# A two-layer block (linear attention and gated MLP, twice) on one core: the hand-written order, engine choices and buffer slots replaced by another set

## Chip, core and metric

The kernel runs on one core of one Trainium2 chip. The core has five engines that run side by side: TensorE (PE, matmuls, with its weight loads PEld), VectorE (DVE), ScalarE (ACT), GpSimd (POOL) and SyncE (SP, which issues DMAs). The metric is the device time of one execution in microseconds (us). Every time below is from the profiler's trace of one execution, or from the timed runs where that is said.

## What is computed

A sequence of 2048 tokens with 512 features goes through attention, MLP, attention, MLP, with the same weights in both layers, everything in bfloat16:

```
x = A_x                                   # (2048, 512)
for layer in (0, 1):
    n = layernorm(x);  q, k, v = split(n @ wqkv)          # 32 heads of 16
    pq, pk = q @ w_phi, k @ w_phi                         # by head, 16 x 16
    phi_q = concat(softmax(pq), softmax(-pq))             # 32 features a head
    phi_k = concat(softmax(pk), softmax(-pk))
    kv = sum over tokens of phi_k x v;  z = sum of phi_k
    x = x + ((phi_q @ kv) / (phi_q @ z + 1e-6)) @ wo
    n = layernorm(x)
    x = x + (relu(n @ W_gate) * (n @ W_up)) @ W_down      # 1376 wide
```

The attention is linear: kv and z need all 16 tiles of keys, and no query can be finished before that. This is the one place in each layer where everything waits for everything.

## The kernel before

**Tiles.** The tokens are 16 tiles of 128 (T). x stays in SBUF in four tensors X0 to X3 for the whole run. The weights are loaded once; w_phi is folded into the key and query weights at the start ("turn", L440, transposes a block of Wk on PE, "wT" copies it, "fold", L448, multiplies it with a block-diagonal w_phi, "W2" copies the result; Wq is transposed by DMA, L435, instead). Both copies are L425 on ACT or L426 on DVE, as are most moves out of PSUM.

**Operations of the first layer, by name and line.** For each tile:

- stats and aggr (L477, L478, DVE), ln and rstd (L485, L487, ACT), xnA (L495, DVE: the normalised tile), xnTA (its transpose: on PE, L466, for the first four tiles, with a copy on ACT; by DMA, L461, for the others).
- K (L535, PE, four matmuls of 128x512): exponentials of plus and minus the result into a buffer ek (L538, ACT, two), sums by head (sk, L546, DVE), one over the sum by lnk and rk (L555, L558, ACT), scaling in two halves, "phi" (L509, on POOL or DVE).
- V (L541, PE, four matmuls) and its copy vext (L425 on ACT or L426 on DVE).
- kvz (L570, PE, eight small matmuls) adds the tile to kv and z in one PSUM buffer q.
- Q (L597, PE, four matmuls), then as for keys: Eq (L600, ACT, two), sq (L603, DVE), lnq and rq (L606, L608, ACT), two halves "phq" (L509, POOL or DVE), and a DMA transpose fq (L611, SP).

When all 16 kvz are done, R and Rz (L582, L587, DVE) build the matrix for the queries. Then, for each tile: erq (L622, PE, eight small matmuls into the same buffer q, which must be free again), lnd and rden (L629 and L633 on ACT, or one reciprocal L631 on DVE), o (L636, DVE), oT (transposed by PE or DMA), proj (L645, PE), resS (L649, DVE: x plus the result), xc (L665, DVE: centred) and xnTB (transposed), ssq (the square's sum, L671 on ACT or L673 on DVE).

The MLP follows in blocks of 1, 1, 2, 4, 4, 2, 2 tiles (1, 1, 2, 4, 4, 2, 1, 1 in the second layer): GU (L698, the last 96 columns), G and Up (L722, PE), rg (L726, ACT: relu), ru (L741 a copy on ACT and then L730 on DVE, or L739 on DVE alone) giving hT, down (L762, PE) and resB (L769, DVE). Tiles of the second layer start their keys while the MLP of the first is still running.

**What sets the order.** Nothing is scheduled at run time. The function builds a list of 1880 operations, ops. ORDER is a list of their numbers: the operations are issued in this order, and each engine takes its own in the order in which they stand there, one after the other. PLACE holds one character for each operation that has a choice of engine, and a "1" swaps it to the other one. SLOTS gives the buffer that each operation takes from its pool: 6 PSUM banks b, one PSUM buffer q, 21 buffers ek, 7 fq, 3 xn and so on. IDLE gives, for the first PE operations, how many idle matmuls of zeros by zeros (L419) stand before each; eight more of them, "warm", begin the program.

```
    order = arrange(ops)
    with tc.manual_schedule():
        fill = iter(IDLE)
        for o in order:
            if o.eng == "PE":
                idle(next(fill, 0))
            o.emit()
```

A wait thus comes from a dependency on another engine, from a buffer that is still in use, or from an instruction ahead on the same engine. DMAs are issued by SP (two at the start by ACT) in order as well; each waits for the landing of the one eight before it.

A number behind a name below counts the operations of that name as they are built (K0 to K15 are the keys of the first layer, K16 to K31 of the second; xnTA has two numbers where PE transposes, one for the matmuls and one for the copy; fold0 to fold3 belong to Wk, fold4 to fold7 to Wq; phi0 and phi1 are the halves of tile 0).

Of the kernel before, what the change touches and what calls it, by code (L numbers as in the profile page):

```python
# [142 lines left out]
class K:  # L143
# [9 lines left out]
    "0101110100000000001100000100110001000011010001111000000011001101010101001001001000101001111111011010"  # L153
    "1011110000000100000001001101000000000111011001011111010111000101001100000101111101001100001101010100"
    "1111111110101010010001000011000100000000101100101010100001001100011100010000110011001101000110111001"
    "010110010110111001110100110100000"
)
SLOTS = (
    "0001425210034050000151131234202310332121143404550125d3104c02302b3020a12113g533004002394131703202e141"
    "5i022124504f013k03583226105214413624335a011h100b033c05053623122j214910170400020501131002000245011020"  # L160
    "2500001142021002010100203200101143020002012105002004314023104g13300215112012320410311e34110200400450"
    "10205113120513d5100i42221240121321402422031200151030231042100142131004133610104f33242541002510104203"
    "51101520500512052130201550414201515300804024k2232c4020121152143124212004023502a533344112050010024104"
    "02024213011055002220j4203h05133317362b222f1506242i013a114023391638231c343e352k221d014g10011500020514"
    "0010124302000012011021450000121302100024010021050012201000011011521101530431102000005112025421011101"
    "0213125200125020013101050032154203115143114220221100253415210511200211401013403005210402213013222420"
    "500210300512431510432512113015114024105320310110512400202"
)
IDLE = (
    0, 0, 0, 0, 0, 0, 0, 0, 0, 0, 2, 0, 4, 0, 0, 0, 0, 0, 0, 0, 0,  # L170
# [708 lines left out]
```

## Time and profile before

| | |
|---|---|
| median of 3 runs | 377.31 us (377.04 to 377.71) |
| span of the profiled execution, first to last instruction | 375.3 us |
| instructions | 7459 |
| PE busy | 364.6 us (97%), 2793 matmul records |
| PEld, DVE, ACT, POOL busy | 216.6 (58%), 285.1 (76%), 209.7 (56%), 93.5 us (25%) |
| granted TensorE clock | 1.000 |
| bytes read from HBM, written | 7.91 MB, 2.10 MB |

The time of the profiled execution is its span and what lies around it; only the span is recorded for it. The median of the timed runs is 2.0 us above this span.

Busy is the union of an engine's instructions over the span. A matmul's record includes its drain, and matmuls overlap, so PE can be busy while it makes no headway; starts in the timeline show that better. Some 40 matmul records are missing (2793 of 2833).

The landings at the start, from the trace (issue, landing, us): X tile 0 0.74, 3.56; first half of Wk 0.74, 4.08; second half 1.19, 4.97; w_phi 1.25, 5.16; wv 1.75, 5.94 and 2.30, 6.74; X tiles 1, 2, 3 2.81 to 3.80, 7.15, 7.50, 7.87; then two tiles (256 KB) each about 0.75 after the last, to 12.36.

### The profile page before, as it was taken

The page shows a single profiled execution, that of the slowest core. Times are in us where ns is not written, and L with a number is a line of the kernel's source. Part 1 is how long each engine was busy: PE and PEld are TensorE (multiplying, and loading weights), DVE is VectorE, ACT ScalarE, POOL GpSimd, SP SyncE. Part 2 cuts the span into 40 slices and gives each one's busy share as a digit, 9 for nine tenths or more (in the row PEclk, how much of TensorE's full clock was granted, in tenths as well). Part 3 has the DMA queues.
Part 4 walks back from the last instruction along what each step waited for, and adds up shares of the span by engine and source line. Part 5 has one row for each costly group of instructions (what it writes and reads, how often), then busy time and mean ns, then how long its engine had stood idle before and what let it go on. Part 6 is the DMA issues. An engine that isn't in the chain of part 4 may idle for free.

```text
span 375.3 us, 7459 instructions
## 1 busy us (share of the span) xinstructions
PE 364.6 (97%) x2793; PEld 216.6 (58%) x2833; DVE 285.1 (76%) x596; ACT 209.7 (56%) x553; POOL 93.5 (25%) x91
## 2 busy tenths in 40 slices
PE   8989997999999999999999999999999999999996
PEld 4534454868554554466476555587745444558585
DVE  6999999999998673685767999999994755543322
ACT  6989999746464532265155499973425323414031
POOL 0377984341010102001004269774000000000000
PEclk9999999999999999999999999999999999999999
DMA  8858844769814221012020102968664120211110
GB/s 256 191 139 175 312 58 85 123 113 132 164 36 84 47 53 31 11 25 56 9 56 2 29 2 57 141 93 142 143 132 85 31 56 2 56 29 51 42 51 30
DMA packets 93444, 31.21 MB, mean 83 GB/s; under 512 B 85248, under 2 KB 92384, under 8 KB 93408
## 3 DMA queue, kind: packets, MB, share of 16 engines
q1 hardware_dynamic: 92992, 30.34, 39.5%
q8 instruction: 22, 0.36, 0.4%
q10 hardware_dynamic: 416, 0.39, 0.3%
q14 instruction: 14, 0.11, 0.1%
HBM read 7.91 MB, written 2.10 MB: 27 GB/s over the span
## 4 chain that ended last, share of the span: by engine, by line
PE 90%; ACT 6%; DVE 1%; POOL 1%; issue 1%; DVEq 0%; another core or an unknown queue 0%
PE b L722 37%; PE b L762 20%; PE b L645 7%; PE b L541 6%; PE b L535 6%; PE b L597 6%; PE b L698 3%; PE q L622 2%; PE q L570 2%; ACT ek L600 1%; POOL ek L509 1%; ACT ek L538 1%; PE q L419 1%; DVE sq L603 1%; ACT hT L425 1%
## 5 line engine op out<-in xcount | busy, mean ns | idle before, releaser
L722 PE MATMUL b<-xnTB,wgu 128*128 128x128 bf16 (+2 forms) x1200 | 149.6, 279 | 0.0
L722 PEld LDWEIGHTS <-wgu 128*128 128x128 bf16 x1200 | 97.1, 98 | 43.6
L509 POOL TENSOR_TENSOR ek<-ek,sk 128x512 bf16<-128x512 bf16 x47 | 51.0, 1109 | 135.5 <-ACT sk L558 108.2
L726 ACT ACTIVATE gu<-b 128x512 bf16<-128x512 f32 (+1 forms) x83 | 47.8, 580 | 64.9 <-PE b L722 64.6
L762 PE MATMUL b<-wd,hT 128*128 128x512 bf16 (+2 forms) x350 | 81.3, 372 | 0.7
L762 PEld LDWEIGHTS <-hT 128*128 128x128 bf16 (+1 forms) x363 | 34.6, 98 | 35.9 <-DVE hT L739 0.2
L509 POOL TENSOR_TENSOR ek<-ek,sq 128x512 bf16<-128x512 bf16 x38 | 42.0, 1127 | 32.6 <-ACT sq L608 18.0
L739 DVE TENSOR_TENSOR hT<-gu,b 128x512 bf16<-128x512 bf16 (+1 forms) x44 | 29.6, 676 | 18.5 <-PE b L722 16.9
L546 DVE TENSOR_REDUCE sk<-ek 128x64 f32<-128x1024 bf16 x32 | 38.7, 1210 | 5.3 <-ACT ek L538 5.2
L538 ACT ACTIVATE ek<-b 128x512 bf16<-128x512 f32 x64 | 35.9, 598 | 9.2 <-PE b L535 8.0
L603 DVE TENSOR_REDUCE sq<-ek 128x64 f32<-128x1024 bf16 x32 | 38.2, 1207 | 0.3 <-POOL ek L509 0.3
L600 ACT ACTIVATE ek<-b 128x512 bf16<-128x512 f32 x64 | 36.1, 623 | 0.6 <-PE b L597 0.5
L730 DVE TENSOR_TENSOR hT<-gu 128x512 bf16<-128x512 bf16 (+1 forms) x39 | 16.7, 429 | 22.5 <-ACT gu L741 22.3
L769 DVE SCALAR_TENSOR_TENSOR X<-b,rsB,X 128x512 bf16<-128x512 f32 (+1 forms) x33 | 23.2, 726 | 13.5 <-PE b L762 13.4
L645 PE MATMUL b<-wo,oT 128*128 128x512 bf16 x118 | 31.2, 379 | 1.2 <-ACT oT L425 0.7
L535 PE MATMUL b<-Wk,xnTA 128*128 128x512 bf16 x122 | 31.4, 379 | 0.3
L541 PE MATMUL b<-wv,xnTA 128*128 128x512 bf16 x124 | 31.0, 379 | 0.4 <-ACT xnTA L425 0.2
L597 PE MATMUL b<-Wq,xnTA 128*128 128x512 bf16 x121 | 30.5, 379 | 0.3
L741 ACT CAST gu<-b 128x512 bf16<-128x512 f32 (+1 forms) x39 | 21.7, 558 | 15.0 <-PE b L722 14.6
L649 DVE SCALAR_TENSOR_TENSOR X<-b,X 128x512 bf16<-128x512 f32 x32 | 21.8, 682 | 3.5 <-PE b L645 3.4
L636 DVE TENSOR_TENSOR o<-q,rd 128x512 bf16<-128x512 f32 x32 | 21.9, 685 | 0.8 <-ACT rd L633 0.6
L477 DVE BATCH_NORM_STATS2 bstA<-X 128x6 f32<-128x512 bf16 x32 | 21.0, 681 | 1.9 <-DMA X<-in_A_x_dram 1.8
(71 smaller groups left out, 349.1 us busy)
## 6 DMA issues: line engine op xcount, KB each, us to landing
out_dram<-X SPq DMA_DIRECT2D x15, 128.0 KB, 1.7
X<-in_A_x_dram SPq DMA_DIRECT2D x6, 256.0 KB, 4.8
wgu<-in_B_W_gate_dram SPq DMA_DIRECT2D x4, 344.0 KB, 4.0
wgu<-in_B_W_up_dram SPq DMA_DIRECT2D x4, 344.0 KB, 3.6
wd<-in_B_W_down_dram SPq DMA_DIRECT2D x5, 256.0 KB, 3.6
wv<-in_A_wqkv_dram SPq DMA_DIRECT2D x2, 256.0 KB, 4.3
wo<-in_A_wo_dram SPq DMA_DIRECT2D x4, 128.0 KB, 3.2
fq<-ek SPq DMA_TRANSPOSE x32, 3.3
```

Of the source, the lines that this page charges most:

```text
L509: e.tensor_tensor(out=out().rearrange("p g s (h f) -> p (g s h) f", f=DH)[:, lo:lo + n], in0=ek.t[:].rearrange("p g s (h f) -> p (g s h) f ...
L535: k = op("PE", mm(4, 512), due, lambda: [nc.tensor.matmul(kp.t[:], lhsT=xnTA[c][:, i, b, :], rhs=Wk2[:, b, :], start=(b == 0), stop=(b == ...
L538: e = [op("ACT", act(512), due, lambda s=s: nc.scalar.activation(out=ek.t[:, :, s, :], in_=kp.t[:].rearrange("p (g e) -> p g e", e=GQ), fu ...
L541: v = op("PE", mm(4, 512), due_v, lambda: [nc.tensor.matmul(vp.t[:], lhsT=xnTA[c][:, i, b, :], rhs=wv[:, b, :], start=(b == 0), stop=(b == ...
L546: a = op("DVE", SUM16, due, lambda: nc.vector.tensor_reduce(out=sk.t[:, row, :], in_=ek.t[:].rearrange("p g s (h f) -> p (g s h) f", f=DH) ...
L597: q = op("PE", mm(4, 512), due, lambda: [nc.tensor.matmul(qp.t[:], lhsT=xnTA[c][:, i, b, :], rhs=Wq2[:, b, :], start=(b == 0), stop=(b == ...
L600: e = [op("ACT", act(512), due, lambda s=s: nc.scalar.activation(out=ek.t[:, :, s, :], in_=qp.t[:].rearrange("p (g e) -> p g e", e=GQ), fu ...
L603: a = op("DVE", SUM16, due, lambda: nc.vector.tensor_reduce(out=sq.t[:], in_=ek.t[:].rearrange("p g s (h f) -> p (g s h) f", f=DH), axis=A ...
L645: a = op("PE", mm(4, 512), due + 3, lambda j=j, yp=yp: [nc.tensor.matmul(yp.t[:], lhsT=oT.t[:, j, b, :], rhs=wo[:, b, :], start=(b == 0), ...
L722: nc.tensor.matmul(ps.t[:, q * W:(q + 1) * W].rearrange("p (i t) -> p i t", t=P), lhsT=wgu[:, s, b, g * P:(g + 1) * P], rhs=xT.t[:, 0:n, b ...
L726: nc.scalar.activation(out=gu.t[:, 0, 0:cols], in_=gp.t[:, 0:cols], func=AF.Relu)
L762: nc.tensor.matmul(yp.t[:, 0:c1 - c0], lhsT=h.t[:m, f * W + i * P:f * W + (i + 1) * P], rhs=wd[:m, f, c0:c1], start=(f == 0), stop=(f == N ...
```

## The change

Only the four constants PLACE, SLOTS, IDLE and ORDER are replaced. The operations, their shapes, the pools and the function that builds them are the same. All of the strings differ; here is their beginning, and IDLE in full (in the changed file the lines below the constants have numbers 3 lower; this text keeps those of the kernel before, but lines quoted from a profile after the change have the new ones):

```diff
 PLACE = (
-    "0101110100000000001100000100110001000011010001111000000011001101010101001001001000101001111111011010"
+    "0101010100000100001100001000110000101110000110000000000110100111000100000000000010001000000001010011"
...
 SLOTS = (
-    "0001425210034050000151131234202310332121143404550125d3104c02302b3020a12113g533004002394131703202e141"
+    "0001245203033002000554133113211224414011381200321310i0311h22300d3403e3120214002k23221c4415a402212041"
...
 IDLE = (
-    0, 0, 0, 0, 0, 0, 0, 0, 0, 0, 2, 0, 4, 0, 0, 0, 0, 0, 0, 0, 0,
+    0, 3, 0, 3, 0,
 )
...
 ORDER = (
-    0, 24, 16, 3, 25, 17, 18, 20, 1, 4, 29, 22, 19, 21, 23, 26, 2, 5, 28, 6, 7, 46, 8, 9, 47, 48, 10, 49, 30, 50,
+    17, 29, 16, 18, 0, 26, 22, 46, 19, 47, 3, 8, 82, 30, 9, 1, 4, 32, 10, 2, 83, 48, 31, 100, 49, 50, 33, 84, 85, 34,
...
```

What the numbers say, worked out from the lists. PE's first groups:

```
before: warm turn0 turn1 turn3 xnTA0 turn2 fold0 fold3 fold1 fold2 (2 idle) V0 K0 (4 idle) xnTA6 xnTA4 xnTA2 V3 K1 K2
        V2 V1 K3 kvz0 fold4 fold6 fold5 fold7 K4 kvz1 V4 V5 K5 kvz3 kvz2 V13 K13 Q3 K12 Q2 V12 kvz5 ...
after:  warm (3 idle) turn0 turn1 (3 idle) turn2 xnTA0 turn3 fold0 fold2 xnTA4 fold1 fold3 xnTA6 V0 V2 V3 K0 xnTA2 fold6
        K3 fold4 K1 fold7 K2 V1 fold5 K5 K4 Q2 Q3 Q1 V4 V12 kvz0 K13 Q0 V13 K12 V5 kvz2 K8 ...
```

PE's groups from the last kvz of the first layer to its first gate group G0:

```
before: kvz11 Q7 Q15 Q10 erq0 Q14 Q9 oT0 proj0 erq1 xnTB0 erq2 oT2 G0
after:  kvz7 Q12 erq0 Q7 Q15 oT0 Q9 proj0 erq1 Q14 xnTB0 oT2 erq2 G0
```

The first DMAs of SP, after the first half of Wk: before w_phi, wv, wv, X tiles 1, 2, 3, then the other 12 tiles in pairs, then four transposes of Wq; after X tiles 2 and 3, w_phi, X tiles 4 and 5, wv, wv, X tile 1, X tiles 12 and 13, two transposes of Wq, four X tiles, two more transposes of Wq, a transpose of an xn, and the last four X tiles. On DVE the zero memset comes first instead of third, and the statistics of tiles 0, 2 and 3 all stand ahead of the first normalisation xnA0, where only tile 0's did.

Engines by PLACE, for the whole program:

| operation | before | after |
|---|---|---|
| vext on ACT / DVE | 19 / 13 | 25 / 7 |
| key halves phi on POOL / DVE | 47 / 17 | 46 / 18 |
| query halves phq on POOL / DVE | 38 / 26 | 51 / 13 |
| lnd and rden on ACT / rden on DVE | 15 / 17 | 19 / 13 |
| ssq on ACT / DVE | 21 / 11 | 17 / 15 |
| ru on ACT / DVE | 39 / 44 | 36 / 47 |
| copies oT, xnTB on ACT / DVE | 8 / 0 | 4 / 4 |
| copies W2 on ACT / DVE | 6 / 2 | 7 / 1 |

In the second layer the last erq of the queries stands after 331.8 us of PE work instead of after 292.9 (by matmul lengths); the last groups of PE (G81, Up81, down90 to down98) are nearly in the same order.

More of the change, by code (lines that the diff above doesn't have):

```diff
@@ L152 @@
 PLACE = (
-    "0101110100000000001100000100110001000011010001111000000011001101010101001001001000101001111111011010"
-    "1011110000000100000001001101000000000111011001011111010111000101001100000101111101001100001101010100"
-    "1111111110101010010001000011000100000000101100101010100001001100011100010000110011001101000110111001"
-    "010110010110111001110100110100000"
+    "0101010100000100001100001000110000101110000110000000000110100111000100000000000010001000000001010011"
+    "0101010111111000110001001100101011011011011010001101001110100001110001111001110110100101001101110111"
@@ L157 @@
+    "1110101111011010101001100000101100000000001000010010101010111101010111010010101000000010100010101000"
+    "101000011011110010110110001101101"
 )
 SLOTS = (
-    "0001425210034050000151131234202310332121143404550125d3104c02302b3020a12113g533004002394131703202e141"
-    "5i022124504f013k03583226105214413624335a011h100b033c05053623122j214910170400020501131002000245011020"
-    "2500001142021002010100203200101143020002012105002004314023104g13300215112012320410311e34110200400450"
-    "10205113120513d5100i42221240121321402422031200151030231042100142131004133610104f33242541002510104203"
@@ L163 @@
[L163 to L167, printed above, removed]
+    "0001245203033002000554133113211224414011381200321310i0311h22300d3403e3120214002k23221c4415a402212041"
@@ new lines @@
+    "0j10011222391007014522263313154g042f26243130103j224a0308351c245b064i215d1000000001121202000202011020"
+    "0400001103021002250100204300101124020000121001000005015313514k44202211112212004023204h51000400310132"
+    "13140053204120841341011112311105115224002023100305123024522315131005f3325451020552316000001210503004"
+    "025225514510201400312000014153021j4210a54215c3321d4200111122102131235124033100e5033i3311040022055001"
+    "0521502324222k2421012342292507144e02523323310g062b2005340702201526030c113g265f301h044922011223020414"
@@ L168 @@
+    "0010101402000203011021240000100202100235010021040010401020031111411500042312103001205510002511311221"
+    "3410422011305400022002101043150250114031034113012232040521110501113011113413403414520120201424302420"
+    "320200300021412520431543115110011220512200000520231542103"
 )
 IDLE = (
-    0, 0, 0, 0, 0, 0, 0, 0, 0, 0, 2, 0, 4, 0, 0, 0, 0, 0, 0, 0, 0,
+    0, 3, 0, 3, 0,
 )
```

181 rows, old and new, of the table ORDER are left out of this document.

## Prediction

> **What bounds the kernel now.** I read first the stages (busy time of each engine by stretch), because the shares of the whole span hide where time is lost. Columns: PE, PEld, DVE, ACT and POOL busy us with their instructions, granted clock, DMA share, GB/s.
>
> ```profile
> 0.00:10.00 10.00, 8.30 (x53) 4.22 (x55) 6.27 (x24) 6.42 (x13) 0.70 (x6) 1.00 0.83 263
> 10.00:20.00 10.00, 9.47 (x72) 4.89 (x71) 9.86 (x21) 9.97 (x31) 4.20 (x4) 1.00 0.87 205
> 20.00:30.00 10.00, 8.57 (x58) 4.11 (x59) 10.00 (x23) 8.77 (x29) 7.44 (x7) 1.00 0.56 135
> 30.00:60.00 30.00, 29.61 (x225) 15.17 (x228) 29.92 (x38) 29.41 (x84) 24.52 (x22) 1.00 0.68 162
> 60.00:65.00 5.00, 3.29 (x46) 2.22 (x45) 4.96 (x8) 4.91 (x18) 2.12 (x2) 1.00 0.54 103
> 65.00:372.00 307.00, 305.26 (x2352) 185.97 (x2382) 223.44 (x486) 150.21 (x384) 54.51 (x50) 1.00 0.34 64
> ```
>
> From 65 us to the last matmul at 372 PE alone is full and sets the time. What can be won lies ahead of 65, where ACT and DVE are as full as PE and PE has holes. Next PE's own waits (total, times, longest):
>
> ```profile
> PE q L570 <- POOL ek L509: 1.5, 3, 0.7
> PE q L419 <- DVE zero L396: 1.3, 1, 1.3
> PE b L466 <- DVE xn L665: 0.8, 1, 0.8
> PE b L645 <- ACT oT L425: 0.7, 1, 0.7
> PE q L622 <- DVE o L636: 0.2, 1, 0.2
> ```
>
> The waits name three places: kvz (L570) behind POOL, the start, and the step from attention to MLP. Busy PE includes the drain of a matmul, so I took the lost time from the starts in the timeline: a 512-column matmul follows the last after 0.216, a 128-column one after 0.056, a kvz or erq one after 0.032; what is longer is lost. That gives 1.34 before the first matmul, 1.7 in the eight warm-up matmuls (0.427 each instead of 0.216), 1.7 in small gaps up to 12.3, 2.3 in kvz between 19.3 and 25.0, and 2.7 between 59.3 and 63.8. After that, nothing over 0.1.
>
> The first gate group (L722, "G0") starts at 64.25. PE work ahead of it: 49 groups of 4x512 at 0.862 = 42.2, 19 of eight kvz/erq at 0.254 = 4.8, 19 of 4x128 at 0.223 = 4.2, 14 warm-up and idle ones at 0.216 = 3.0; sum 54.2. So **10.0 us are lost ahead of G0**, and this is the number that the change must alter.
>
> **Why they are lost.** For ACT, DVE and POOL I take as an instruction's engine time the stretch from the end of the one before it to its own end, averaged over the trace (the timeline shows four exponentials L538 in 2.04, four casts L425 in 2.05: 0.51 each). ACT work up to the cast that G0 reads, in the kernel's order: 32 exponentials of keys 16.4, 32 of queries 16.0, 16 pairs lnk/rk 6.1, 9 pairs lnq/rq 3.0, 11 vext casts 5.6, 6 casts of Wk/Wq 2.9, 10 other casts 5.1, 10 ln/rstd pairs 3.4, table and two DMA issues 2.2, two lnd/rden 0.7, one square 0.7: 62.1. ACT idle before that: 0.74, 1.58 (for the first statistics) and 0.2, so 2.5. Sum 64.6, against 64.25 seen. ACT sets G0; the kvz gaps and the long chain at 59 lie in its shadow in part.
>
> **The change, part by part.** It removes and adds no matmul: the same 2833, six of them idle, and the same 54.2 ahead of G0. Counts that do move: vext on ACT 19 to 25, rden/lnd on ACT 15 to 19, square on ACT 21 to 17, relu copies on ACT 39 to 36, query halves (phq) on POOL 38 to 51, key halves 47 to 46. By the engine times explained above, DVE's whole work falls from 285 to 277 and ACT's from 211 to 209; POOL's rises by 12.6.
>
> *Front.* Three idle matmuls now precede the first transpose and three the third. The zero memset is first on DVE (0.27 earlier), so: warm-up 1.15 to 4.54, three idle ones to 5.35, first transpose 5.35 instead of 4.72, its cast (L425) 5.74 instead of 5.22. Its weights landed at 4.1, so these idles cost ACT 0.9 of idle in place of 0.2. On DVE the statistics of two more tiles stand before the first normalisation (L495, at 5.09 before); their loads are moved to second and third on SP, where the trace's landings (256 KB each 0.75) put them near 4.9 and 5.3. So L495 comes at 6.5 and its transpose at 7.0, not 5.56; ACT meanwhile has casts to do and stays busy. ACT idle becomes 3.4. On SP the moved loads pull wv to about 7 and 7.7 (5.9, 6.7 before); V0 starts near 9.8 by ACT's casts, so that is hidden. Two later X loads stand behind Wq's transposes and an xnTA transpose; the queries of early tiles now fill PE there.
>
> *kvz.* kvz0 goes from PE's 22nd group to its 33rd, behind three queries. POOL's first half waits for rk0: ACT sum 11.9 + 2.5 = 14.4 before (seen: 14.5), now 18.5 + 3.4 = 21.9. Two halves end at 24.0, when PE has just reached kvz0. The 2.3 lost in kvz go, but the later POOL start is paid below.
>
> *ACT up to G0.* 24 exponentials of queries instead of 32 (-4.0), 6 lnq/rq pairs (-1.0), one lnd/rden (-0.4), no square (-0.7), 13 vext (+1.0), 7 W casts (+0.5): 57.5, with 3.4 idle 60.9, so 6.7 lost. The tightest place is two groups earlier: proj0 has 51.5 of PE work and 55.3 of ACT before it, 58.7, so **7.2 lost**. DVE up to the first centred tile falls from 59.6 to 53.8 and is no bound.
>
> *The step to MLP.* Before, proj0 follows its transpose at once, and xnTB0 follows proj0 after one erq (0.25), though L649 and L665 take 1.1; seen: 0.84, 1.0, and 0.36 and 0.34 beside. Now a query group (0.86) stands in each of these places; the same rows leave 0.2 at xnTB0 and 0.2 to 0.4 at oT1/erq2.
>
> *POOL.* Up to the second half that erq1's transpose needs, POOL now does 31 halves without a rest: 21.9 + 31 x 1.04 + 2.0 of waits for ACT's rk/rq (running sum) = 56.2, and 3.3 for the DMA transpose: 59.5. erq1 has 52.4 of PE work before it: 7.1 lost, the same as ACT. But POOL has no slack left for this:
>
> ```profile
> 20.86 4.10 POOL L509 TENSOR_TENSOR ek<-ek,sk 128x512 bf16<-128x512 bf16 x4 [1.02 <-ACT sk L558]
> ...
> 39.12 4.62 POOL L509 TENSOR_TENSOR ek<-ek,sk 128x512 bf16<-128x512 bf16 x4
> 41.12 0.68 DVE L509 TENSOR_TENSOR ek<-ek,sk 128x512 bf16<-128x512 bf16 x1
> ```
>
> Four halves take 4.10, and 4.62 where DVE starts the same operation just ahead of one of them; single POOL halves go from 1.057 to 1.36 to 1.57 there. Five DVE halves now stand among POOL's last ten before erq1. None hit: 0; all hit: 5 x 0.5 = 2.5; I take two, 1.0. [...]
>
> *Later stages.* For each PE group after G0 I compared the PE work between it and the group it depends on with the durations of the chain between. Before, this finds 0.16 short in all, and no wait is seen. Now it finds 0.27, the largest 0.15 at an erq in the second layer. I cost it at 0.1. The last groups, the last resB and the store are the same: 0.
>
> **Sum.** Lost ahead of G0: 7.2 (ACT) to 8.1 (POOL with two hits); I take 7.7. Gain 10.0 - 7.7 = 2.3; the later 0.1 is within rounding. The profiled span 375.3 becomes 373.0; the median of the runs, 377.31, is 2.0 above the span, which I keep: **375.0**.
>
> **Rivals.**
> 1. *The front slips.* If the two tiles' loads land where their predecessors did (7.15, 7.50), L495 is at 7.9, 1.4 later, and the first xnTA cast stops ACT for 1.0 to 1.4. For it: the DMA engines are 0.83 busy in the first 10 us. Against: only 640 KB stand ahead of them, which had landed by 4.97. 376.2.
> 2. *No change.* ACT idles 2 more than I count, since its order now alternates between keys and queries that wait for each other: lost 9.5 to 10. 376.8 to 377.3.
> 3. *Slower: POOL becomes the bound.* Before, it had 9.5 of idle between 14.5 and 60; now none. If halves take 1.20 (between 1.057 and 1.565) instead of 1.04, 31 of them put fq1 5.0 later, 12.1 lost: 379.4. It decides from 1.13 a half, where POOL gives 10.0. For it: page mean 1.109 and 1.127 for one. Against: that mean overlaps its neighbour, and DVE does fewer halves than before (6 instead of 9 up to there).
>
> **Numbers.** Forecast (373.8 to 375.7) 0.58; rival 1 0.18; rival 2 0.11; rival 3 0.13. Below: ACT's sum alone, 7.2 lost and its idle 0.6 smaller, gives 373.9, and 0.3 for the match of that sum to the trace gives 373.6. Above: rival 2's end, 377.3. A change under 0.2% (376.6 to 378.1) can't be told from none here: faster 0.76, same 0.11, slower 0.13.
>
> **What would show it.** Right: no wait of kvz on POOL before 30; G0 near 62; POOL's first half near 22; lost time at proj0, xnTB0 and erq2 under 1 together; PE without gaps after G0. Wrong: L495's first at 7.9 (rival 1); erq on fq as the longest wait, POOL halves over 1.13 (rival 3); a new PE wait after 65, which the chains above do not foresee.

## The result and the profile after

The changed kernel takes **395.93 us** (median of four runs, 392.82 to 396.02) beside 377.26 (377.04 to 377.71) for the kernel before on the same chip: ratio 1.047, 95% interval 1.0445 to 1.049. It is slower by 18.7 us, where 375.0 was forecast. Its profiled execution is the quickest of the four, 392.82 us, with a span of 391.0; the other three have spans of 394.1 to 394.2 at a granted clock of 0.987 instead of 0.995 (see the clock, below).

The same stretches of the changed kernel as were shown of before (the busy time of PE, PEld, DVE, ACT and POOL with their instructions, granted clock, DMA share, GB/s):

```profile
0.00:10.00 10.00, 8.17 (x59) 4.56 (x61) 5.62 (x19) 5.73 (x15) 0.70 (x6) 1.00 0.89 239
10.00:20.00 10.00, 9.89 (x61) 5.13 (x61) 9.69 (x27) 10.00 (x28) 0.00 (x0) 1.00 0.81 195
20.00:30.00 10.00, 8.43 (x47) 3.89 (x46) 10.00 (x19) 9.29 (x27) 8.30 (x8) 1.00 0.71 174
30.00:60.00 30.00, 25.78 (x214) 13.32 (x216) 29.95 (x30) 25.33 (x77) 26.46 (x24) 0.99 0.54 142
60.00:65.00 5.00, 4.68 (x26) 2.22 (x26) 4.26 (x7) 1.96 (x6) 2.89 (x3) 0.71 0.55 105
65.00:372.00 307.00, 295.69 (x2198) 175.45 (x2231) 231.26 (x465) 144.78 (x397) 70.00 (x63) 1.00 0.34 60
```

PE lost time in two places: between 20 and 60 (4.2 of 30 us idle in the fourth stretch, where it was 0.4), and, which no step had foreseen, after 65 (11.3 idle instead of 1.7). DVE is full from 20 to 60 with only 30 instructions in the fourth stretch, where 38 filled it before: **fewer operations, each longer**. The matmuls are the same, and the last one starts at 387.6 instead of 371.8, so PE lost 15.8 us more. Counting only gaps of over a quarter of a us between starts, its lost time is about 22 us in all (7 before; the prediction's 10.0 also counts the slow warm-up and smaller gaps). G0 starts at 68.47 (64.25 before), and from there to the end of the last matmul it is 319.4 us (307.9).

PE's own waits (total, times, longest):

```profile
PE q L567 <- DVE ek L506: 2.2, 2, 1.2
PE q L567 <- DVE vext L423: 2.0, 2, 1.3
PE b L532 <- DVE vext L423: 1.5, 1, 1.5
PE q L619 <- DVE o L633: 1.5, 3, 1.1
...
PE b L759 <- DVE hT L736: 1.2, 1, 1.2
...
PE q L567 <- POOL ek L506: 0.5, 1, 0.5
```

Before, the longest was kvz behind POOL. That one is nearly gone (0.5 instead of 1.5), as forecast; in its place PE waits for DVE: for key halves, vext, o and hT. What made DVE late is seen in its timeline from 22.9 us on (start, length, engine, line, operation, number merged), first DVE, then POOL:

```profile
22.89 0.65 DVE L492 TENSOR_SCALAR xn<-X,mvA,rsA 128x512 bf16<-128x512 bf16 x1
23.45 1.27 DVE L474 BATCH_NORM_STATS2 bstA<-X 128x6 f32<-128x512 bf16 x2
24.65 2.03 DVE L492 TENSOR_SCALAR xn<-X,mvA,rsA 128x512 bf16<-128x512 bf16 x2
26.59 1.01 DVE L410 TENSOR_TENSOR Mg<-Mf 128x4 f32<-128x4 f32 x1
```

```profile
21.31 8.30 POOL L506 TENSOR_TENSOR ek<-ek,sk 128x512 bf16<-128x512 bf16 x8 [20.00 <-ACT sk L555]
```

Two normalisations take 2.03 us, and a product of 128x4 elements takes 1.01, while POOL runs eight halves without a rest; the statistics between them take their usual 0.64. At 51.57 it is worse: five key halves on DVE, on which the last kvz of the layer wait, take 6.91 us (0.64 each would be 3.2):

```profile
51.57 6.91 DVE L506 TENSOR_TENSOR ek<-ek,sk 128x512 bf16<-128x512 bf16 x5
```

To count this over the whole run I took each DVE operation's time from the end of the one before it (or its own start) to its end, less its time where nothing meets it (half 0.60, normalisation 0.33, centring 0.27, hT from SBUF 0.33, the small ones of Mg, lnB and sqB 0.09), and call it **held** where over 0.15 is left:

| | held operations | us held | of it in the first 120 us | time, us |
|---|---|---|---|---|
| before | 8 | 3.2 | 0.7 | 377.3 |
| after | 41 | 25.4 | 13.8 | 395.9 |

The same is seen in the profile's groups, whose means are those of the whole records; first before, then after (the last numbers are total us, mean ns, idle before):

```profile
L495 DVE TENSOR_SCALAR xn<-X,mvA,rsA 128x512 bf16<-128x512 bf16 x32 | 12.7, 421 | 1.3 <-ACT rsA L487 1.2
L509 DVE TENSOR_TENSOR ek<-ek,sk 128x512 bf16<-128x512 bf16 x17 | 11.8, 708 | 1.2 <-ACT sk L558 1.2
```

```profile
L492 DVE TENSOR_SCALAR xn<-X,mvA,rsA 128x512 bf16<-128x512 bf16 x32 | 18.4, 593 | 1.8 <-ACT rsA L484 1.8
L506 DVE TENSOR_TENSOR ek<-ek,sk 128x512 bf16<-128x512 bf16 x18 | 17.7, 1016 | 0.2 <-ACT sk L555 0.2
```

The longest hold in the changed kernel is 0.93, under one POOL half (1.06). Reductions (1.13 to 1.14, with and without POOL's halves), statistics (684 ns a record, 681 before), copies out of PSUM (vext 677, 680 before) and the sums that read PSUM (resS 684, 682 before) are as long as before.

**The clock.** The changed kernel has one stretch at half clock that the kernel before has not, 59.5 to 62.9, right behind the longest stalls; matmuls of 512 columns follow one another there by 0.427 us instead of 0.216, which costs 1.7.

```profile
56.00:59.00 3.00, 0.80 (x19) 0.64 (x18) 3.00 (x3) 1.82 (x5) 3.00 (x3) 1.00 0.06 19
59.00:63.00 4.00, 3.68 (x20) 1.64 (x18) 3.92 (x7) 1.03 (x3) 3.89 (x4) 0.57 0.20 40
```

PE was busy for 0.80 of the 3.00 us ahead of it, and the stretch is 3.4 long. What makes the clock fall is not shown here: from 246 to 248 PE was busy for 0.68 of 2.00 us both in this run and in that of experiment 4, and from 248 to 250 the clock was 1.00 here and 0.55 there. A run of 394.2 at 0.987 spends 2 x 0.013 x 394.2 = 10.2 us at half clock, the profiled one 2 x 0.005 x 391 = 3.9 (estimates from the granted clocks). The difference of 6.3 costs up to 3.2, which is what separates their spans. Where the further stretches lie is seen in experiment 4, whose profiled run has 0.987 too: 57.0 to 63.9 and 248.2 to 251.6, 10.2 us together, both behind stalls of PE (busy for 0.73 of 2.00 from 55 to 57, and 0.68 as above). So the clock adds 1.7 to 5 us to the stalls, and in these two traces its stretches stand behind them. In the traces of experiments 6, 9 and 11 below, where PE loses less, no such stretch is left between the warm-up and the last matmul (granted clock 1.000, 0.999 and 1.000).

### The profile page after: what moved, and what is told of

Read it like the earlier page. It is cut to its first block, busy times and chain, and to the rows that moved or that the text cites. A ratio compares the mean times of both kernels' runs of the same rounds, so it can differ in the third digit from the quotient of the medians.

```text
span 391.0 us, 7388 instructions
## 1 busy us (share of the span) xinstructions
PE 368.4 (94%) x2789; PEld 217.3 (56%) x2833; DVE 298.9 (76%) x585; ACT 201.6 (52%) x553; POOL 108.4 (28%) x103
## 4 chain that ended last, share of the span: by engine, by line
PE 60%; DVE 19%; issue 5%; ACT 2%; DMA 1%; DVEq 0%
PE b L719 30%; PE b L759 15%; PE b L642 5%; DVE ek L506 5%; PE b L594 4%; DVE sk L543 2%; PE b L695 2%; DVE sq L600 2%; PE q L619 2%; DVE X L766 1%; DVE o L633 1%; DMA oT<-o 1%; DVE hT L736 1%; DVE X L646 1%; DVE bstA L474 1%
## 5 line engine op out<-in xcount | busy, mean ns | idle before, releaser
L719 PE MATMUL b<-xnTB,wgu 128*128 128x128 bf16 (+2 forms) x1200 | 153.1, 279 | 0.9 <-DVE X L766 0.5
L506 POOL TENSOR_TENSOR ek<-ek,sq 128x512 bf16<-128x512 bf16 x51 | 56.3, 1126 | 134.8 <-ACT sq L605 72.4
L759 PE MATMUL b<-wd,hT 128*128 128x512 bf16 (+2 forms) x344 | 84.0, 372 | 3.4 <-DVE hT L736 1.2
L506 POOL TENSOR_TENSOR ek<-ek,sk 128x512 bf16<-128x512 bf16 x46 | 51.7, 1150 | 52.4 <-ACT sk L555 48.8
L736 DVE TENSOR_TENSOR hT<-gu,b 128x512 bf16<-128x512 bf16 (+1 forms) x47 | 31.6, 676 | 24.3 <-PE b L719 16.9
L543 DVE TENSOR_REDUCE sk<-ek 128x64 f32<-128x1024 bf16 x32 | 37.9, 1206 | 0.5
L594 PE MATMUL b<-Wq,xnTA 128*128 128x512 bf16 x122 | 32.0, 390 | 0.5 <-issue 0.2
L633 DVE TENSOR_TENSOR o<-q,rd 128x512 bf16<-128x512 f32 x32 | 21.9, 686 | 9.0 <-ACT rd L630 8.7
L738 ACT CAST gu<-b 128x512 bf16<-128x512 f32 (+1 forms) x36 | 19.6, 556 | 14.4 <-PE b L719 14.4
```

What stands on the lines that cost most here:

```text
L506: e.tensor_tensor(out=out().rearrange("p g s (h f) -> p (g s h) f", f=DH)[:, lo:lo + n], in0=ek.t[:].rearrange("p g s (h f) -> p (g s h) f ...
L543: a = op("DVE", SUM16, due, lambda: nc.vector.tensor_reduce(out=sk.t[:, row, :], in_=ek.t[:].rearrange("p g s (h f) -> p (g s h) f", f=DH) ...
L594: q = op("PE", mm(4, 512), due, lambda: [nc.tensor.matmul(qp.t[:], lhsT=xnTA[c][:, i, b, :], rhs=Wq2[:, b, :], start=(b == 0), stop=(b == ...
L719: nc.tensor.matmul(ps.t[:, q * W:(q + 1) * W].rearrange("p (i t) -> p i t", t=P), lhsT=wgu[:, s, b, g * P:(g + 1) * P], rhs=xT.t[:, 0:n, b ...
L736: nc.vector.tensor_tensor(out=h.t[:, f0 * W:f0 * W + cols], in0=gu.t[:, 0, 0:cols], in1=up.t[:, 0:cols], op=Alu.mult)
L759: nc.tensor.matmul(yp.t[:, 0:c1 - c0], lhsT=h.t[:m, f * W + i * P:f * W + (i + 1) * P], rhs=wd[:m, f, c0:c1], start=(f == 0), stop=(f == N ...
```

## Experiments

**Theories.** A: POOL's halves hold up some of VectorE's operations (halves, normalisations, small products), and the planned order has no slack for it; what makes one engine wait for the other no run shows, and "the port" in the expectations below is no more than the author's name for it. B: the new order, slots and late kvz lose the time by themselves. C: the clock. D, formed later: POOL's pace alone.

### 1. The halves' engines put back

46 of PLACE's characters, those of phi and phq; its first line:

```diff
-    "0101010100000100001100001000110000101110000110000000000110100111000100000000000010001000000001010011"
+    "0101010100000100001100001100110000001010010000110000000010000111010101001001001000101001111111010011"
```

> The changed kernel with one part undone: only the engine choices of the feature halves (keys and queries) are those of the kernel before; order, slots, front idles and all other choices stay changed. POOL loses 12 to 14 halves (of 97), 11 of them queries of the first layer. Theory A (POOL's denser stream of halves holds up VectorE's own operations, and these reach PE as waits): VectorE's normalisations (593 ns each in the changed kernel, 421 before) come back under 480, PE's lost time ahead of the first gate group falls by 4 us or more, time 379 to 387. Theory B (the new order, slots and late kvz lose the time, whatever engine does a half): 392 to 396, within 0.5% of the changed kernel, with the waits of kvz and K still there. Theory C (the half-clock window near 60 us is the cause): the window goes only if the stalls ahead of it go, and is worth 1.7 to 3 us by itself.

405.63 us (ratio 1.076, 1.073 to 1.079). A miss for A as I had put it, and for B. The normalisations stayed long (546 ns by the count above, 518 in the changed kernel, 349 before), and 33 operations were held for 18.4 us although POOL did no more halves than in the kernel before, where 8 were held. So it is not the number of POOL's halves that counts. What it is instead is taken up by experiment 12.

### 2. The halves' engines alone

The same characters of the changed kernel in the kernel before.

> The kernel before with this one part alone: the engine choices of the feature halves are those of the changed kernel; order, slots and all else are of the kernel before. Theory A: VectorE is held up as in the changed kernel (normalisations over 500 ns), 384 to 392. Theory B: the order of before keeps its slack, 376 to 379.

387.77 us (1.028, 1.025 to 1.031): this part alone costs 10.5, inside A's range. But the normalisations, for which I had given over 500, stay at 353; 17 operations are held for 9.6 us, most of them halves and hT. PE now waits for vext on DVE (3.1) and for hT (1.4). How much of the 10.5 is holds was not tested here.

### 3. All engine choices put back

The whole of PLACE is that of the kernel before.

> The changed kernel's order, slots and front idles, with all engine choices (halves, value casts, squares, ReLU copies, reciprocals) of the kernel before. Theory A: VectorE's and POOL's loads are again those of before, so most of the loss goes: 377 to 384. Theory B: 390 to 396. Between 384 and 390 both have a share, or an order and its engine choices only work together.

428.4 us (1.135, 1.134 to 1.137), beyond what either theory gave. 25 operations are held there for 16.5 us, fewer than in the changed kernel, and still it is 32.5 us slower than that. An order and its engine choices are one plan, and with another plan's choices it falls apart. As a way to undo a part, experiments 1 and 3 tell nothing clean; that is why the following ones leave the plan as it is and change what an operation does.

### 4. Without the front idles

```diff
-    0, 3, 0, 3, 0,
+    0, 0, 0, 0, 0,
```

> The changed kernel without its six idle matmuls at the front. Theories A and C: within 1 us of the changed kernel (392 to 396), the first transpose 0.65 us earlier and the loss unchanged. Theory B in its form 'the front idles push the whole chain': 393 or less, by the 0.65 to 1.3 us that the idles take, and no more, so they can't be the cause of 18 us.

393.53 us (391.79 to 394.99): the idles are not the cause. Its runs differ by the clock, as in the changed kernel: spans 389.9 and 390.4 at 0.996, 393.1 twice at 0.987. Against runs of the changed kernel at nearly the same clock (391.0, and 394.1 to 394.2) this is 0.6 to 1.1 less; the rest of the 2.4 between the medians is the clock.

### 5. The two engines by themselves

> Nothing of the kernel but its VectorE and GpSimd operations, each on tiles of its own, so that no data ties the two engines; the output is the input copied. In stages: GpSimd alone; VectorE alone; both, with GpSimd issuing halves (128x512), quarters (128x256) or very small memsets without a pause. Theory A: beside GpSimd's halves VectorE's normalisation (350 to 420 ns in the kernel before) and its feature half (640 ns) take up to one GpSimd half longer, 1.0 us or more each, beside quarters about half of that, beside small memsets under 0.1 us more; reduction, statistics and the operations that read PSUM stay within 5% of their time alone. Theory B: VectorE's operations stay within 15% of their time alone whatever GpSimd does.

Four stages of the trace, mean ns of one:

| VectorE operation | alone | beside POOL halves | beside quarters | beside small memsets |
|---|---|---|---|---|
| normalisation (SBUF to SBUF) | 413 | 1135 | 580 | 412 |
| half (two inputs in SBUF) | 690 | 1239 | 913 | 690 |
| product of 4 columns (two in SBUF) | 159 | 329 | 350 | 159 |
| reduction by head | 1219 | 1217 | 1216 | 1217 |
| statistics | 693 | 692 | 692 | 692 |
| copy from PSUM | 688 | 687 | 686 | 687 |

First alone, then beside halves, in the profile's groups (operation, tiles, shapes, number, total us, mean ns, idle before):

```profile
L40 DVE TENSOR_TENSOR hd<-ekd,sk 128x512 bf16<-128x512 bf16 x6 | 4.1, 690 | 0.2
...
L45 DVE TENSOR_SCALAR xn<-x,mv,rs 128x512 bf16<-128x512 bf16 x6 | 2.5, 413 | 23.7 <-SPq L83 23.5
```

```profile
L40 DVE TENSOR_TENSOR hd<-ekd,sk 128x512 bf16<-128x512 bf16 x4 | 5.0, 1239 | 0.1
L48 DVE TENSOR_REDUCE red<-ekd 128x64 f32<-128x1024 bf16 x4 | 4.9, 1217 | 0.1
L45 DVE TENSOR_SCALAR xn<-x,mv,rs 128x512 bf16<-128x512 bf16 x4 | 4.5, 1135 | 0.2
```

No data ties the two engines here, and still a normalisation goes from 0.41 to 1.14. B is refuted; A has the right kinds of operation, and a size that is too large (0.7 to 0.8 longer, where it had given 1.0 or more). The first of the four halves was not held and took 600 by the count above, the other three 1425 to 1427 (691 to 693 each alone). The other direction, which is the one that I had priced, is smaller: a POOL half goes from 1.055 alone to 1.38 beside a VectorE half, once 1.58. What holds these three kinds up by 0.2 to 0.7 us on average and leaves reductions, statistics and copies from PSUM within 0.002 us of their time alone is not shown by these runs.

### 6 and 7. Short holds, in both kernels

```diff
-                    "POOL": ("POOL", (1016, 1058), lambda k=k: phi(nc.gpsimd, k * H, H), 3)}
+                    "POOL": ("POOL", (1016, 1058), lambda k=k: small(k * H), 3)}
...
+        def small(lo):
+            phi(nc.gpsimd, lo, 1)
+            for _ in range(4):
+                nc.gpsimd.memset(tiny[:], 0.0)
+            phi(nc.gpsimd, lo + H - 1, 1)
```

> The changed kernel with each of GpSimd's 97 halves replaced by six very small operations of about the same total time (two products of 16 columns at its two ends, which keep the waits and the order, and four memsets of 4 columns between); 30 of the 32 groups of 16 columns of such a half are left unscaled. [...] Theory A: VectorE's normalisations and halves come back to 0.41 and 0.69 us or less, VectorE's busy time falls by 15 us or more, and the time to 374 to 381. Theory B: 388 to 396, the order itself is short. Between 381 and 388 both have a share.

> The kernel before with the same replacement of GpSimd's 85 halves. Theory A and B: little is lost to the port there, so 374 to 377.5; the edit by itself is worth no more than 3 us. If it is worth more, the last run does not stand for the change alone.

The changed kernel: **374.36 us** (ratio to before 0.992, 0.991 to 0.994), the kernel before: 377.86 (1.0018, 1.0007 to 1.0029). The first is inside A's range. The edit takes 21.6 from the one and adds 0.5 to the other (377.32 beside it; 0.4 over the range given). VectorE's busy time in the changed kernel falls from 298.9 to 274.2. But POOL's replacement took 0.95 us a half on average where the real halves took 1.11, so POOL was also quicker; the next two runs separate the two effects.

### 9 and 10. The same at the real pace, and slower

```diff
-            for _ in range(4):
+            for _ in range(5):
```

and 6 in experiment 10.

> As the run without long holds, with five small memsets in place of four: GpSimd's pace was 0.86 us from half to half there, faster than the 1.015 of real halves, so that run took away some of GpSimd's time as well as its holds. Now 1.02 by that run's trace (0.16 a memset), the pace of real halves that meet nothing; 30 of 32 groups of a GpSimd half stay unscaled. Theory A (the holds): within 2 us of that run, 374 to 377. Rival D (GpSimd's pace: it had no slack, and the earlier run was quick because GpSimd was): 380 or more, with erq waiting on the transposed features.

> The same with six small memsets: 1.18 us from half to half, slower than the real halves of the changed kernel with their collisions (1.11 mean). Theory A: if GpSimd's pace counts at all it shows here: 375 to 381, and far under the 393 to 396 of the changed kernel. Rival D: 390 or more. The third rival of the prediction (halves of 1.20 us give 379.4) is measured by this run.

A half's time on POOL is counted here from the start of its first operation (or the end of the half before it) to the end of its last, with the pauses between.

| changed kernel | POOL, mean us a half, and sum | held operations | us |
|---|---|---|---|
| real halves | 1.110, 107.7 | 41 | 395.9 |
| four memsets | 0.952, 92.4 | 0 | 374.4 |
| five memsets | 1.104, 107.1 | 0 | 377.2 (376.5 to 377.9) |
| six memsets | 1.261, 122.3 | 0 | 384.3 |

With five memsets POOL works as long as in the changed kernel, 107.1 us against 107.7, and the time is 377.21: it is the holds on VectorE, **18.7 us between the medians, 15.6 to the profiled execution's own time**, clock included, and not POOL's own time. A had given 374 to 377, within 2 of experiment 6, and missed by 0.2 and 0.9: D has a share; from 0.95 to 1.10 a half the time goes up by 2.9, from there to 1.26 by 7.1. The 384.3 of six memsets lies between A's range (375 to 381) and D's (390 or more), which says the same. In the run with five memsets:

```profile
48.80 3.14 DVE L507 TENSOR_TENSOR ek<-ek,sk 128x512 bf16<-128x512 bf16 x5
```

```profile
PE q L417 <- DVE zero L394: 1.2, 1, 1.2
PE q L574 <- POOL ek L507: 1.1, 2, 0.6
PE b L649 <- DMA oT<-o: 0.9, 1, 0.9
PE b L726 <- ACT rd L637: 0.5, 1, 0.5
```

The five key halves are back at 3.14 (6.91), and of PE's waits for DVE only the one for the first memset is left at the head of the list.

### 8. Halves as two quarters

```diff
-lambda k=k: phi(nc.gpsimd, k * H, H), 3)}
+lambda k=k: [phi(nc.gpsimd, k * H + j, H // 2) for j in (0, H // 2)], 3)}
```

> The changed kernel with each of GpSimd's halves done as two quarters of 256 columns: the same work and result, a hold of the port of 0.62 us in place of 1.06 (as GpSimd ran them alone), but 2 x 0.58 in place of 1.02 us from one to the next, 14% more of GpSimd. Theory A: the mean normalisation falls from 593 to under 500 ns and the time to 382 to 393. Theory B: no gain from shorter holds, and GpSimd is later: 394 to 403.

395.69 us: inside B's range (394 to 403), but not for B's reason alone. POOL took 1.26 a half here, and the six memsets of experiment 10, as slow and without a hold, take 384.3, so 11.4 are left for the holds. Most holds did shrink: the normalisations fall from 518 to 445 (whole records 593 to 515, where A had under 500), and but for one no hold is over 0.47 (0.93 with halves). That one took the gain back:

```profile
51.53 13.34 DVE L506 TENSOR_TENSOR ek<-ek,sk 128x512 bf16<-128x512 bf16 x5
```

```profile
50.31 2.37 POOL L506 TENSOR_TENSOR ek<-ek,sq 128x256 bf16<-128x256 bf16 x4
52.63 3.51 POOL L506 TENSOR_TENSOR ek<-ek,sk 128x256 bf16<-128x256 bf16 x6
56.09 5.83 POOL L506 TENSOR_TENSOR ek<-ek,sq 128x256 bf16<-128x256 bf16 x10
```

```profile
L506 DVE TENSOR_TENSOR ek<-ek,sk x5: 677/679/10934, 51.5 to 64.2; 128x512 bf16<-128x512 bf16 x5
```

```profile
PE q L567 <- DVE ek L506: 8.5, 2, 8.3
```

The first of these two lines gives the shortest, middle and longest of the five in ns. POOL runs 20 quarters without a pause from 50.31 to 61.92. The first of the five VectorE halves, started at 51.53, takes 10.93 us and ends 0.5 after POOL stops; the other four take 0.68 each. PE stands still for 8.3.

### 11. Short holds in the first layer only

```diff
-lambda k=k: phi(nc.gpsimd, k * H, H), 3)}
+lambda k=k: small(k * H) if l == 0 else phi(nc.gpsimd, k * H, H), 3)}
```

Here l is the layer, and small is that of experiment 9.

> As with five memsets, but only in the first layer's 54 GpSimd halves; the second layer's 43 are real. Theory A, by PE's lost time in the changed kernel (about 13 of its 22 us ahead of 120 us and 8 after, against 7 and 0 before): the first layer's part goes and the second's stays, 381 to 386. Rival E (all of it comes from the first layer's late start, the second only inherits it): 374 to 378.

382.73 us (381.84 to 384.20), inside A's range: no operation is held in the first 120 us, 20 are later (11.1 us). By the medians the first layer's holds cost 395.9 - 382.7 = 13.2, the second's 382.7 - 377.2 = 5.5.

### 12. Experiment 1 again, with short holds

> The first experiment (changed kernel, engine choices of the halves as before), which went to 405.6 and so against theory A as it was stated, now with GpSimd's 85 halves as two small products and five small memsets, 1.10 us mean as in the run at the same pace; 30 of 32 groups of a GpSimd half stay unscaled. Theory A in its second form (what counts is where VectorE's operations meet GpSimd's, not how many halves GpSimd does; VectorE's 13 more halves add 8 us of work of its own): the holds go here too, 379 to 390. Theory B for that run (these choices don't fit the new order, with or without holds): 398 to 405.

392.56 us (392.1 to 393.3), between the two ranges. Of experiment 1's loss of 28.4 the holds make 13.1; the other 15.3 are not holds. PE's kvz waits there for POOL (3.4 in two waits, 2.2 in four) and for vext on DVE (1.8): choices that this order was not laid out for. B is right for this mixture, but not for the changed kernel.

## Why the prediction was wrong, step by step

- **What bounds the kernel before**: the 10.0 us ahead of G0 stand. ACT's account of them (62.1 of work, 2.5 of idle) meets 64.25 partly by luck, since its durations are averages over the whole trace. Added up over those instructions alone, the same trace gives 59.7 of work and 4.5 of idle, 1.1 of it ahead of a value cast at 26.22 that the account leaves out.
- **Front**: right. POOL's first half came at 21.3 (21.9 forecast), the first transpose at 5.39 (5.35), the first xnTA at 7.16 (7.0); kvz's waits for POOL are down from 1.5 to 0.5. Rival 1 is out: the first normalisation starts at 6.70 (6.5 forecast, 7.9 for the rival).
- **POOL's and ACT's sums**: POOL's is right where nothing is held. With five memsets erq1 starts at 59.24 (59.5 forecast) and G0 at 61.46 (54.2 + 7.7 = 61.9). In the changed kernel they start at 65.52 and 68.47. ACT's is no floor: with four memsets G0 starts at 59.87, ahead of the 60.9 that ACT was to allow, and with four, five and six it moves with POOL, 59.87, 61.46, 66.26. In the run with five ACT works 54.8 up to the cast that G0 reads (57.5 forecast) and idles 6.6 (3.4); that its total came out right is luck again, two errors that cancel.
- **The step that failed: "DVE up to the first centred tile falls from 59.6 to 53.8 and is no bound."** I multiplied the changed counts by durations from a run in which VectorE and POOL hardly met (8 operations held, 3.2 us), so the sum carried over a favourable timing as if it were a property of the operations. Up to and with the first centring DVE's instructions take 59.6 us in the changed kernel and 51.7 in the run with five memsets (each from the end of the one before, idle left out), so the term was 5.8 too small, and 7.9 are the difference that the holds make; that centring ends at 67.3 and at 60.3. The whole of DVE's work was to be 277; it is 298.9 with the holds and 274.5 without. I looked at collisions, but from POOL's side alone (5 x 0.5, of which I took 1.0). The five VectorE halves "among POOL's last ten before erq1" are those of the 6.91 us. All five were met: POOL's halves beside them took 1.50 instead of 1.05, and they cost DVE 3.7, and kvz, R and all that follows wait for them. Only one side of a collision was priced; experiment 5 shows 0.68 to 0.83 on VectorE's side for 0.33 to 0.53 on POOL's.
- **"Later stages +0.1"**: wrong twice. The same durations stood in the chain check, and the second layer's holds cost 5.5. Without any hold the stretch from G0 to the last matmul is still 311.0 us (307.9 before), 3.1 more, with PE waiting for an oT by DMA (1.1 at 258), for a gate group (0.65 at 81) and in a kvz (0.7 at 231). These 3.1, less 0.4 for the earlier G0, are why the run without holds gives 377.2 (377.5 in its profiled execution) and not 375.0, to about half a us. So at the mean pace that POOL had in the changed kernel, its own collisions included, this plan is no quicker than the one before even unheld. At the 1.02 to 1.06 of a real half that meets nothing, a line between four and five memsets gives 375.6 to 376.4 (an estimate).
- **Rivals 2 and 3**: rival 2 (ACT idles more) has the 377.2 of the run without holds in its range, but by another way: the 9.5 to 10 lost ahead of G0 that it needs are 7.3 there (61.46 - 54.2), and the rest is lost behind G0. Rival 3 (POOL becomes the bound) has the right sign, but the 18.7 us are not POOL's own time: its mean of 1.11 stayed below the 1.13 from which I let it decide. Without holds POOL's pace does move G0, as above. The rival's price was a little low: 379.4 for 1.20, where a line between the measured points gives 381.5 (an estimate).
- **What would show it wrong**: "a new PE wait after 65" was on the list and came; it should have had a price and a chance, which it could only have had from VectorE's side of the collisions.

What stays open: which of a plan's meetings of VectorE and POOL are the costly ones could only be read from the traces, not changed one by one. The kernel before was run with four memsets only, not with five. A version that beats both kernels came out only with most of the scaling left out, so no such version is offered.

## What to carry to other kernels

A duration from a trace holds for the neighbours it had there. Where a change moves work between two engines that hold each other up, take each operation's time alone and its time when it is met, from both sides (here 0.41 and 1.14 for a normalisation, 1.06 and 1.38 for a POOL half), and count the meetings of the new order before calling an engine "no bound". To test a suspected hold, keep the plan and the pace and take only the hold away; putting back one part of a fitted plan mixes the suspect with a misfit.

## Not expected of the hardware

- A product of 4 columns took 0.93 us instead of 0.09 by the count above (Mg at 26.59): a hold of 0.84, where the longest of any operation in that run, on a half (0.60 when nothing meets it), is 0.93. With POOL's quarters (0.62 alone, a half 1.06) in experiment 8 holds are up to 0.47, but for one.
- In experiment 8 one VectorE half was held for 10.3 us behind some 18 POOL quarters in a row, though beside POOL's halves no hold is longer than 0.93. What decides it is not known from these runs.
- POOL's memsets of 4 columns and products of 16 columns in quick succession held nothing up that could be measured (no operation over 0.15 in experiments 6, 9 and 10).
